# An attention and gated-convolution kernel on one core: loads held back by a second pass of its planner, memsets, weight conversion and small column copies put elsewhere

## The chip, the cores and the metric

The kernel runs on one core of a Trainium2 chip. The core has a matrix engine (PE, TensorE), three engines for elementwise work (DVE, the VectorE; ACT, the ScalarE; POOL, the GpSimd), and SP, the SyncE, whose queue issues nearly all of the DMAs here. Every engine works through its own instructions in order and waits at semaphores for the others. The metric is the device time of one execution in microseconds (us).

## The reference

Two stages, for a batch of 4 with 12800 rows of 128 numbers each, float32. An attention through 49 agents, and a gated convolution over its output:

```python
def sm(a, b):
    s = scale * (a @ b.transpose(0, 2, 1))
    s = s - s.max(-1, keepdims=True)
    e = np.exp(s)
    return e / (e.sum(-1, keepdims=True) + 1e-09)
agent_v = sm(agents, k) @ v          # 49 x 128 for each batch
x = sm(q, agents) @ agent_v          # 12800 x 128
# gated convolution, 5 taps that look back in the sequence
for t in range(5):
    gate_pre += conv_w[t][None, None, :] * xp[:, t:t + S, :]   # xp: 4 zero rows, then x
gate = 1.0 / (1.0 + np.exp(-gate_pre))
out = (gate * (x @ w_val)) @ w_out
```

The three weight arrays come in one array `moe`, whose numbers are float64; the kernel loads it as pairs of 32-bit words and makes float32 of it by integer operations.

## The kernel before

**Tiling.** A batch is cut into 10 units of 1280 rows (40 units in all), two units are a segment of 2560 columns, and the convolution runs over 100 chunks of 512 columns (the last is done in two halves). For a unit of keys, PE makes scores (`key_scores`, L401, matmuls L381), ACT copies them from PSUM to `ks` (L407), and DVE takes their maxima (`kmx`, L416). When all ten units of a batch are there, `key_max` makes one bias from the maxima, ACT takes exponentials (L476), DVE transposes them in blocks (`eT`, L391), and PE sums the values with them (`av`, L485). `fold_weights` then multiplies the agents' values into the weights of the convolution (`gw` L546, `wst`, `stat`), so that x itself is never formed: PE multiplies the attention weights with folded matrices.

**Queries.** For a unit of queries (`queries`), PE makes scores (L381), DVE transposes them (`sT`) and takes maxima (`qmx`), POOL subtracts (`qw` L755), ACT takes exponentials (L763), DVE sums and normalises (L768 to L777). The result goes to `pt` as float16 pieces: the high part (ACT L784), a repeated part (POOL L790) and the low part (POOL L798). `pt` is then transposed into a segment buffer `x1` (named x_0 to x_3 in traces) by a DMA transposition (L839; the first four units by PE, L853). The first four columns of a segment are the last four of the segment before; POOL copies them (`halo`, L823, or zeroes them at the start of a batch, L820).

**The fourth part, x2.** Nineteen of the 49 rows have a second low part for which `x1` has no room. Their five shifted copies are copied by two DMAs (`shifts`, L888) from rows of `x1` into `x2`, which has 128 partitions of 2560 columns with the 95 copied rows from partition 32 on; the partitions around them have to be zero, and POOL zeroes them once at the start (L275, L276).

**A chunk.** `gates`: five matmuls for the taps (L926) and one for x2 (L930), then a tanh on ACT (L939). `values`: two matmuls (L953, L957), then `h` on DVE (L966), its float16 part `hh` on ACT (L972) and the rest `hl` on POOL (L977). `project`: three matmuls (L996, L997 on `hh`, L998 on `hl`), a scaled copy on ACT (L1010), and for each pair of chunks a DMA to the output (L1025).

**What sets the order.** PE's order is a list written out by hand (`order`, L1092). Every other engine's order comes from `Plan`: each step is added with its engine, an estimated duration and the keys that it reads and writes; `Plan.order` (L96) replays the program once with these durations and, where several steps of an engine could run, takes the one with the longest tail of work behind it. DMAs are steps too; the ones on SP's queue stand there in the order of their planned starts. Loads go into a ring of eleven buffers (`load`, L359): a load may be planned as soon as the work on the load eleven places earlier is done. The weights (`weights`, L284) are one DMA and 13 operations on DVE; `urge=1e3` puts the DMA ahead of everything.

## Time and profile before

| | |
|---|---|
| time, three runs | 425.37, 426.81, 592.71 us; median 426.81 us |
| profiled execution: time, span | 425.08 us, 423.0 us |
| busy: PE, DVE, ACT, POOL | 400.9, 302.1, 301.5, 250.3 us |
| mean granted TensorE clock | 0.987 |
| moved by DMA | 127.63 MB, mean 302 GB/s |

The profile is one execution. Its span reaches from the first to the last instruction; the execution's own time is 2.08 us longer. A row of a timeline gives the start, the duration, the engine, the line, what is written from what, and in brackets how long the engine had been idle before and what ended that. A row of the waits gives the engine and line that waited, who released it, the sum in us, how often, and the longest. A row of the windows gives busy time and number of instructions for PE, its weight loads, DVE, ACT and POOL, then the granted PE clock, the DMA share and GB/s. SPq stands for SP's queue: the duration there is that of issuing the DMA, not of the transfer.

### The profile page before, as it was taken

Reading aid. Unit: us, or ns where it says so; the run is one execution under the profiler, and the core shown is the slowest. Engines: PE = TensorE matmul, PEld = TensorE weight load, DVE = VectorE, ACT = ScalarE, POOL = GpSimd, SP = SyncE. Lnnn points to the kernel's source line nnn. Section 1 sums busy time; section 2 is a strip of 40 time slices with the busy share of each in tenths; the row PEclk is TensorE's granted clock in tenths of the full one; section 3 lists DMA queues with packets and bytes.
Section 4 is the critical chain, followed back from the end, with each engine's and each line's share of the span. In section 5 each row is a group of like instructions: output and inputs, shape, how many; then the busy total and the mean of one; then the engine's idle time right before and its main releaser. Section 6 shows DMA issues by size and latency. Waiting matters only on the chain.

```text
span 423.0 us, 10093 instructions
## 1 busy us (share of the span) xinstructions
PE 400.9 (95%) x3907; PEld 194.3 (46%) x3907; DVE 302.1 (71%) x566; ACT 301.5 (71%) x521; POOL 250.3 (59%) x309
## 2 busy tenths in 40 slices
PE   4769999999999999999999999999999899999996
PEld 2239444336555443445555444344555444344443
DVE  6978899876885978676796775758766568676231
ACT  2446558779957677678886686779876467788776
POOL 9502558665677566555577564655476267887553
PEclk9969999999999999999999999999999989999999
DMA  8999999999999999999999999999999967655633
GB/s 319 417 418 413 352 381 363 293 323 311 414 317 288 376 350 340 377 284 307 362 350 316 319 229 364 309 310 254 318 415 315 235 177 168 192 164 176 198 128 124
DMA packets 75130, 127.63 MB, mean 302 GB/s; under 512 B 50466, under 2 KB 50850, under 8 KB 75084
## 3 DMA queue, kind: packets, MB, share of 16 engines
q1 hardware_dynamic: 74940, 126.87, 95.2%
q8 instruction: 30, 0.49, 0.6%
q10 hardware_dynamic: 144, 0.13, 0.2%
q14 instruction: 16, 0.13, 0.1%
HBM read 79.25 MB, written 26.21 MB: 249 GB/s over the span
## 4 chain that ended last, share of the span: by engine, by line
PE 81%; DVE 11%; DMA 3%; ACT 2%; POOL 2%; issue 1%; POOLq 0%; DVEq 0%
PE gate L926 24%; PE sc L381 18%; PE av L485 9%; PE val L953 5%; PE out L996 5%; PE gate L930 5%; PE val L957 5%; PE out L997 5%; PE out L998 5%; DVE ob L301 2%; DVE kmx L416 2%; DMA x<-pt 2%; DVE qw L777 1%; DVE h L966 1%; DMA ob<-moe 1%
## 5 line engine op out<-in xcount | busy, mean ns | idle before, releaser
L977 POOL TENSOR_TENSOR hl<-h,hh 128x512 f16<-128x512 f32 (+1 forms) x101 | 116.8, 1158 | 85.6 <-ACT hh L972 85.5
L926 PE MATMUL gate<-x,stat 128*128 128x512 f16 (+1 forms) x500 | 125.3, 381 | 0.4 <-ACT th L939 0.2
L966 DVE SCALAR_TENSOR_TENSOR h<-th,val 128x512 f32<-128x512 f32 x100 | 67.8, 678 | 62.9 <-PE out L997 27.0
L381 PE MATMUL sc<-ld,ag_sb 128*32 128x320 f32 x1280 | 102.0, 447 | 9.6 <-DMA ld<-kT 8.9
L939 ACT ACTIVATE th<-gate,unscale 128x512 f32<-128x512 f32 x100 | 68.5, 685 | 30.7 <-PE gate L930 29.4
L1010 ACT ACTIVATE ob<-out,oscale 128x512 f32<-128x512 f32 x98 | 67.4, 688 | 22.2 <-PE out L998 21.7
L926 PEld LDWEIGHTS <-stat 128*128 128x128 f16 x505 | 46.3, 98 | 63.7 <-issue 14.4
L972 ACT CAST hh<-h 128x512 f16<-128x512 f32 (+1 forms) x101 | 61.7, 611 | 15.9 <-DVE h L966 15.5
L381 PEld LDWEIGHTS sc<-ld,ag_sb 128*32 128x32 f32 x1280 | 36.5, 111 | 61.5 <-issue 25.2
L755 POOL TENSOR_TENSOR qw<-sT,qmx 128x490 f32<-128x490 f32 x40 | 41.4, 1035 | 34.8 <-DVE qmx L750 34.7
L485 PE MATMUL av<-ld,eT 128*32 128x129 f32 (+1 forms) x1400 | 48.0, 274 | 0.0
L485 PEld LDWEIGHTS av<-ld,eT 128*32 128x32 f32 (+1 forms) x1400 | 44.4, 113 | 6.9 <-issue 2.5
L798 POOL TENSOR_TENSOR pt<-qw,pt 128x490 f16<-128x490 f32 x40 | 44.8, 1120 | 1.0 <-ACT pt L784 0.8
L407 ACT COPY ks<-sc 128x640 f32<-128x640 f32 x40 | 27.6, 691 | 23.7 <-PE sc L381 18.4
L391 DVE STREAM_TRANSPOSE sT<-sc 128x640 f32<-128x640 f32 x40 | 33.5, 837 | 13.0 <-PE sc L381 12.3
L476 ACT ACTIVATE e<-ks,kbias 128x320 f32<-128x320 f32 x80 | 39.2, 555 | 3.0 <-DVE kbias L462 1.9
L998 PE MATMUL out<-hl,wo 128*128 128x512 f16 x98 | 37.1, 379 | 2.5 <-POOL hl L977 2.5
L790 POOL TENSOR_SCALAR pt<-qw 128x240 f16<-128x240 f32 x80 | 27.5, 365 | 20.0 <-DVE qw L777 20.0
L391 DVE STREAM_TRANSPOSE eT<-e 128x640 f32<-128x640 f32 x40 | 33.3, 839 | 7.5 <-ACT e L476 4.7
L953 PE MATMUL val<-x,stat 128*128 128x512 f16 x100 | 37.9, 379 | 0.2 <-DVE wo L733 0.2
L930 PE MATMUL gate<-x,stat 128*128 128x512 f16 x100 | 38.0, 380 | 0.0
L957 PE MATMUL val<-x,stat 128*128 128x512 f16 x100 | 37.8, 378 | 0.0
(132 smaller groups left out, 432.9 us busy)
## 6 DMA issues: line engine op xcount, KB each, us to landing
ld<-kT SPq DMA_DIRECT2D x40, 640.0 KB
ld<-qT SPq DMA_DIRECT2D x40, 640.0 KB
ld<-vP SPq DMA_DIRECT2D x39, 645.0 KB
outT<-ob SPq DMA_DIRECT2D x48, 512.0 KB
x<-x SPq DMA_DIRECT2D x18, 325.0 KB
x<-x SPq DMA_DIRECT2D x18, 150.0 KB
outT<-ob SPq DMA_DIRECT2D x3, 256.0 KB
x<-x SPq DMA_DIRECT2D x4, 162.5 KB
```

Of the source, the lines that this page charges most:

```text
L381: nc.tensor.matmul(out=out[g * BLK : (g + 1) * BLK, j, 0:GT], lhsT=ag_sb[:, b, j * BLK : (j + 1) * BLK], rhs=src[:, g * GT : (g + 1) * GT] ...
L391: nc.vector.transpose(out=out.rearrange("p n (j i) -> p j n i", j=2), in_=in_.rearrange("p j (n i) -> p j n i", i=BLK),)
L485: nc.tensor.matmul(out=av[o + j : o + j + cols, 0 : C + 1], lhsT=et[:, n, j : j + cols], rhs=vt[:, n, :], start=(u == 0 and n < 2), stop=( ...
L926: nc.tensor.matmul(out=pg, lhsT=stat[:, k, :], rhs=x1[:, c : c + w], start=(k == 0), stop=False,)
L930: nc.tensor.matmul(out=pg, lhsT=stat[:, TAPS + 1, :], rhs=x2[:, o2 : o2 + w], start=False, stop=True,)
L939: lambda: nc.scalar.activation(out=th, in_=pg, func=AF.Tanh, scale=unscale[:, 0:1]),
L953: nc.tensor.matmul(out=pv, lhsT=stat[:, TAPS, :], rhs=x1s[(b * NCH + n0 // CH) // 5 % NX][:, PAD + o2 : PAD + o2 + w], start=True, stop=False,
L957: nc.tensor.matmul(out=pv, lhsT=stat[:, TAPS + 2, :], rhs=x2[:, o2 : o2 + w], start=False, stop=True,)
L966: lambda: nc.vector.scalar_tensor_tensor(out=h, in0=th, scalar=1.0, in1=pv, op0=ALU.add, op1=ALU.mult),
L972: "act", 0.16 + 0.42 * scale, lambda: nc.scalar.copy(out=hh, in_=h),
L977: lambda: nc.gpsimd.tensor_tensor(out=hl, in0=h, in1=hh, op=ALU.subtract),
L1010: lambda: nc.scalar.activation(out=ob[:, o : o + w], in_=po, func=AF.Copy, scale=oscale),
```

## The change

Five edits, in the planner and in what is planned.

1. **Held loads.** `Plan.order` replays twice. From the first replay it takes, for each load, the earliest planned start of a step that uses it; in the second replay the load can't start earlier than `HOLD` = 13 planned us before that. PE's order stays as it was, row for row.
2. **Row copies of 12 and 7.** The nineteen rows of x2 are cut into 12 (first 2, every 4) and 7 (first 0, every 4) in place of 13 (first 0, every 4) and 6 (first 6, every 8); the two copies have 60 and 35 rows of five shifts in place of 65 and 30. The six further repeated rows of `pt` become 28, 32 to 48.
3. **Preceding columns later.** `halo` of a segment is added behind the POOL work on `pt` of that segment's second unit (it reads that key), no longer right behind the copies of the segment before.
4. **x2 zeroed elsewhere.** DVE zeroes the first 32 partitions as 32-bit words, ACT the last 32 by copying a zero column; both are planned steps. POOL's six memsets are gone.
5. **Weights behind values.** The DMA of `moe` loses its `urge`, and the 13 operations are planned with 0.43 us each.

**DVE, from the transpositions of the last exponentials to the fold of batch 0.** `eT` is the transposition whose result the value matmuls wait for, `ob` the buffers in which the weights are converted, `qsm`, `qr`, `qw` a unit of queries, `av2`, `den`, `avT` the fold. Before:

```order
L391 STREAM_TRANSPOSE eT1_83<-e1_81 128x2x10x32
L391 STREAM_TRANSPOSE eT2_84<-e0_80 128x2x10x32
L391 STREAM_TRANSPOSE eT0_82<-e1_81 128x2x10x32
L768 TENSOR_REDUCE qsm0_93<-qw0_89 128x10
L769 SCALAR_TENSOR_TENSOR qsm0_93<-qsm0_93,tiny_146 128x10
L772 RECIPROCAL qr0_95<-qsm0_93 128x10
L777 TENSOR_TENSOR qw0_89<-qw0_89,qr0_95 128x490
L524 COPY av2_169<-av_139 128x129
L539 TENSOR_SCALAR den_170<-out_138 128x49
L540 RECIPROCAL den_170<-den_170 128x49
L541 TENSOR_TENSOR avT_171<-out_138,den_170 128x49
```

Now:

```order
L412 STREAM_TRANSPOSE eT0_82<-e1_81 128x2x10x32
L322 TENSOR_SCALAR ob1_121<-ob0_120 128x261
L798 TENSOR_TENSOR qw0_89<-qw0_89,qr0_95 128x490
L337 CAST ob1_121<-ob1_121 128x261
L322 TENSOR_SCALAR ob1_121<-ob1_121 128x261
L339 SCALAR_TENSOR_TENSOR ob1_121<-ob1_121 128x261
L545 COPY av2_165<-av_139 128x129
L343 TENSOR_TENSOR ob1_121<-ob1_121 128x261
L322 TENSOR_SCALAR ob1_121<-ob0_120 128x261
L560 TENSOR_SCALAR den_166<-out_138 128x49
L561 RECIPROCAL den_166<-den_166 128x49
L562 TENSOR_TENSOR avT_167<-out_138,den_166 128x49
```

The conversion (rows on `ob`) stood ahead of and among the keys' maxima, at the start of DVE's program; now five of its 13 operations stand between the last `eT` rows just ahead of this piece, four ahead of `av2`, two between `av2` and `avT`, and the last two behind `avT`.

**POOL, around the second segment of batch 3.** `pt0` and `pt1` are the two units of a segment, `x1_0` its buffer, `x1_3` the segment before, `hl` what the chunks' last matmul waits for. Before:

```order
L790 TENSOR_SCALAR pt0_97<-qw0_89 128x10x24
L790 TENSOR_SCALAR pt0_97<-qw0_89 128x10x6
L798 TENSOR_TENSOR pt0_97<-qw0_89,pt0_97 128x10x49
L823 COPY x1_0_101<-x1_3_104 128x4
L977 TENSOR_TENSOR hl0_117<-h0_111,hh0_114 128x512
L977 TENSOR_TENSOR hl1_118<-h1_112,hh1_115 128x512
L546 TENSOR_TENSOR gw_173<-avT_171,moe_sb_167 128x245
L755 TENSOR_TENSOR qw1_90<-sT1_86,qmx1_88 128x490
L977 TENSOR_TENSOR hl2_119<-h2_113,hh2_116 128x512
```

Now:

```order
L819 TENSOR_TENSOR pt0_97<-qw0_89,pt0_97 128x10x49
L998 TENSOR_TENSOR hl1_118<-h1_112,hh1_115 128x512
L567 TENSOR_TENSOR gw_169<-avT_167,moe_sb_163 128x245
L776 TENSOR_TENSOR qw1_90<-sT1_86,qmx1_88 128x490
L998 TENSOR_TENSOR hl2_119<-h2_113,hh2_116 128x512
L710 TENSOR_SCALAR wo_172<-moe_sb_163,unscale1_131 128x128
L998 TENSOR_TENSOR hl0_117<-h0_111,hh0_114 128x512
L819 TENSOR_TENSOR pt1_98<-qw1_90,pt1_98 128x10x49
L811 TENSOR_SCALAR pt1_98<-qw1_90 128x10x24
L811 TENSOR_SCALAR pt1_98<-qw1_90 128x10x6
L846 COPY x1_0_101<-x1_3_104 128x4
```

The copy of the preceding columns has moved from ahead of two `hl` to behind the work on `pt1`, past four `hl`.

**SP's queue, at a transposition in batch 1.** `ld` are the ring's buffers, `x1_3<-pt2` is the transposition of the same unit in both. Before:

```order
L374 DMA ld0_61<-qT 128x1280
L1025 DMA outT<-ob2_122 128x1024
L888 DMA x20_105<-x1_2_103 65x1x2560
L888 DMA x20_105<-x1_2_103 30x1x2560
L374 DMA ld1_62<-kT 128x1280
L374 DMA ld2_63<-kT 128x1280
L374 DMA ld3_64<-qT 128x1280
L1025 DMA outT<-ob3_123 128x1024
L839 DMA_TRANSPOSE x1_3_104<-pt2_99 128x10x128
L374 DMA ld4_65<-vP 128x1290
```

Now:

```order
L909 DMA x20_105<-x1_2_103 60x1x2560
L909 DMA x20_105<-x1_2_103 35x1x2560
L395 DMA ld8_69<-kT 128x1280
L1046 DMA outT<-ob3_123 128x1024
L860 DMA_TRANSPOSE x1_3_104<-pt2_99 128x10x128
L395 DMA ld9_70<-kT 128x1280
L395 DMA ld10_71<-qT 128x1280
L1046 DMA outT<-ob0_120 128x512
L395 DMA ld0_61<-qT 128x1280
L860 DMA_TRANSPOSE x1_3_104<-pt3_100 128x10x128
```

Before, the loads up to buffer 3 stand ahead of this transposition and the next is that into buffer 4; now the next is that into buffer 9, which is six loads less ahead.

The diff:

```diff
--- before.py
+++ after.py
@@ -34,8 +34,8 @@
 NDUP = 30
 X2R = 19
 X2B = 32
-FOURS = 13
-X2CUTS = ((0, FOURS, 0, 4, 0.45), (FOURS, X2R, 6, 8, 0.25))
+FOURS = 12
+X2CUTS = ((0, FOURS, 2, 4, 0.45), (FOURS, X2R, 0, 4, 0.25))
 
 
 NLOAD = 11
@@ -61,6 +61,7 @@
 BACKLOG = 3.0
 LANES = 8
 LAND = 1.4
+HOLD = 13
 
 QS = 256.0
 WS = 64.0
@@ -76,11 +77,13 @@
 
 
     def __init__(self):
-        self.steps, self.urge = [], []
+        self.steps, self.urge, self.early = [], [], {}
         self.wrote, self.read = {}, {}
 
-    def add(self, engine, us, fn, reads=(), writes=(), moved=0.0, key=None, urge=0.0):
+    def add(self, engine, us, fn, reads=(), writes=(), moved=0.0, key=None, urge=0.0, early=None):
         i = len(self.steps)
+        if early is not None:
+            self.early[i] = early
         need = set()
         for x in reads:
             need |= self.wrote.get(x, set())
@@ -94,6 +97,15 @@
         self.urge.append(urge)
 
     def order(self):
+        self.replay({})
+        users = {i: [] for i in self.early}
+        for j, s in enumerate(self.steps):
+            for i in s[3]:
+                if i in users:
+                    users[i].append(self.start[j])
+        return self.replay({i: min(users[i]) - self.early[i] for i in users})
+
+    def replay(self, hold):
         n = len(self.steps)
         after = [[] for _ in range(n)]
         last = None
@@ -116,7 +128,7 @@
         wire = 0.0
         lanes = [0.0] * LANES
         left = [len(s[3]) for s in self.steps]
-        at = [0.0] * n
+        at = [hold.get(i, 0.0) for i in range(n)]
         queues = {e: [] for e in engines}
         pe = [i for i, s in enumerate(self.steps) if s[0] == "pe"]
         here = 0
@@ -261,6 +273,7 @@
     fold = const.tile([P, AP_], F32, name="fold")
     ag_sb = const.tile([P, B, AP_], F32, name="ag_sb")
     tiny = const.tile([P, NBLK], F32, name="tiny")
+    zero = const.tile([P, 1], F16, name="zero")
     nc.scalar.dma_start(out=ag_sb, in_=agT)
     make_identity(nc, ident)
     make_identity(nc, ident16)
@@ -271,9 +284,7 @@
     nc.vector.memset(x1s[0][:, 0:PAD], 0.0)
     for t in wst_sb:
         nc.gpsimd.memset(t[:, TAPS + 1 :, :], 0.0)
-    for t in x2s:
-        nc.gpsimd.memset(t[0:X2B], 0.0)
-        nc.gpsimd.memset(t[P - BLK :], 0.0)
+    nc.vector.memset(zero, 0.0)
 
     moe_sb = const.tile([P, NW], F32, name="moe_sb")
     wval_sb = moe_sb[:, 0:C]
@@ -284,8 +295,18 @@
     def weights():
 
 
+        for i, t in enumerate(x2s):
+            keys = [("x2", i, h, c[0]) for h in (0, UNIT) for c in X2CUTS]
+            add("dve", 1.4, lambda t=t: nc.vector.memset(t[0:X2B].bitcast(I32), 0), (), keys)
+            add(
+                "act", 2.0,
+                lambda t=t: nc.scalar.copy(
+                    out=t[P - BLK :], in_=zero[P - BLK :].to_broadcast([BLK, SEG])
+                ),
+                (), keys,
+            )
         if moe.dtype == F32:
-            add("dma", 0.4, lambda: nc.sync.dma_start(out=moe_sb, in_=moe), (), ["moe"], 0.4, urge=1e3)
+            add("dma", 0.4, lambda: nc.sync.dma_start(out=moe_sb, in_=moe), (), ["moe"], 0.4)
         else:
 
             i0, i1 = (t.bitcast(I32) for t in obs[0:2])
@@ -336,10 +357,10 @@
                 lambda: nc.sync.dma_start(
                     out=raw, in_=moe.bitcast(I32).rearrange("p (n two) -> p n two", two=2)
                 ),
-                (), ["raw"], 0.65, urge=1e3,
+                (), ["raw"], 0.65,
             )
             for fn in ops:
-                add("dve", 0.35, fn, ["raw"], ["bits"])
+                add("dve", 0.43, fn, ["raw"], ["bits"])
             add("dve", 0.43, whole, ["bits"], ["moe"] + [("ob", i, o) for i in range(2) for o in (0, CH)])
         add(
             "dve", 0.13,
@@ -372,7 +393,7 @@
         for d, f, keys in parts:
             add(
                 "dma", 0.4, lambda d=d, f=f: nc.sync.dma_start(out=d, in_=f), (), keys,
-                1.57 / len(parts),
+                1.57 / len(parts), early=HOLD,
             )
 
     def score_matmuls(b, src, out):
@@ -579,16 +600,16 @@
         ghi = wst[:, 0:TAPS, 0:A]
         vhi = wst[:, TAPS, 0:A]
 
-        def pick(x, first, every):
-            return x[:, first:A:every] if len(x.shape) == 2 else x[:, :, first:A:every]
+        def pick(x, first, every, n):
+            return (x[:, first:A:every] if len(x.shape) == 2 else x[:, :, first:A:every])[..., 0:n]
 
         def lows(low, full, hi, less):
 
 
             for out, first, every, n in (
-                (low[0], 1, 2, ODD), (low[1], 2, 8, NDUP - ODD), (low[2], 0, 4, FOURS), (low[3], 6, 8, X2R - FOURS),
+                (low[0], 1, 2, ODD), (low[1], 28, 4, NDUP - ODD), (low[2], 2, 4, FOURS), (low[3], 0, 4, X2R - FOURS),
             ):
-                less(out, pick(full, first, every), pick(hi, first, every))
+                less(out, pick(full, first, every, n), pick(hi, first, every, n))
 
         def rest(out, full, s, hi):
             dve.scalar_tensor_tensor(
@@ -786,9 +807,9 @@
         )
 
         def again():
-            for o, n, first, every in ((2 * A, ODD, 1, 2), (2 * A + ODD, NDUP - ODD, 2, 8)):
+            for o, n, first, every in ((2 * A, ODD, 1, 2), (2 * A + ODD, NDUP - ODD, 28, 4)):
                 nc.gpsimd.tensor_scalar(
-                    out=pt[:, :, o : o + n], in0=w[:, :, first : A - 1 : every],
+                    out=pt[:, :, o : o + n], in0=w[:, :, first : A : every][:, :, 0:n],
                     scalar1=1.0, scalar2=0.0, op0=ALU.mult, op1=ALU.add,
                 )
 
@@ -800,6 +821,9 @@
             ),
             [("qw", g % NPT), (*p_, 0)], [(*p_, 1)],
         )
+        if g % 2 and g > SINGLE + 1:
+            halo(g // 2, [(*p_, 1)])
+
     def on_pe(b, u):
         g = b * NU + u
         return g < PE_FIRST or (g < (B - 1) * NU and g % TURN in PE_TURNS)
@@ -814,19 +838,16 @@
         i = s % NX
         return [(x, i, h) for h in halves for x in ("x1", "x1b")] + [("x1h", i)] * (0 in halves)
 
-    def halo(s):
+    def halo(s, read=()):
         to = x1s[s % NX][:, PAD - HALO : PAD]
         if s * 2 % NU == 0:
             fn = lambda: nc.gpsimd.memset(to, 0.0)
-            read = []
         else:
             fn = lambda: nc.gpsimd.tensor_copy(
                 out=to, in_=x1s[(s - 1) % NX][:, PAD + SEG - HALO : PAD + SEG]
             )
-            read = [(x, (s - 1) % NX, 1) for x in ("x1", "x1b")]
-
-        read.append(("x2", (s - 1) % 3, UNIT, 0))
-        add("pool", 0.1, fn, read, [("x1h", s % NX)])
+        keys = [(x, (s - 1) % NX, 1) for x in ("x1", "x1b")]
+        add("pool", 0.19, fn, list(read) + keys, [("x1h", s % NX)])
 
     def transposes(b, u):
         g = b * NU + u
@@ -891,8 +912,8 @@
                 ),
                 src, [("x2", s % 3, o + i * UNIT, r0) for i in range(n)], us * n,
             )
-        if g % 2 and (g + 1) // 2 < B * NU // 2:
-            halo((g + 1) // 2)
+        if g % 2 and g < SINGLE:
+            halo(g // 2 + 1)
 
 
     chunks = [(t // NCH, t % NCH * CH, CH) for t in range(NT - 1)]
```

## The prediction

> **What bounds the kernel now.** The page's busy line and the chain of work that ended last say PE:
>
> ```profile
> PE 400.9 (95%) x3907; PEld 194.3 (46%) x3907; DVE 302.1 (71%) x566; ACT 301.5 (71%) x521; POOL 250.3 (59%) x309
> PE 81%; DVE 11%; DMA 3%; ACT 2%; POOL 2%; issue 1%; POOLq 0%; DVEq 0%
> ```
>
> PE's order is the same row for row after the change, so its work is the same, and only its idle time and its clock can move. The table of windows shows where it idles (first number behind the length: PE's busy time):
>
> ```profile
> 0.00:30.00 30.00, 17.46 (x186) 7.17 (x188) 23.48 (x34) 10.88 (x17) 15.20 (x16) 0.89 0.96 383
> 30.00:40.00 10.00, 10.00 (x186) 10.00 (x184) 9.21 (x15) 7.59 (x16) 1.02 (x1) 1.00 1.02 414
> 40.00:60.00 20.00, 17.83 (x207) 8.35 (x203) 16.64 (x45) 10.48 (x18) 11.57 (x20) 1.00 1.00 366
> 60.00:330.00 270.00, 269.52 (x2863) 130.78 (x2861) 202.19 (x375) 204.99 (x357) 165.48 (x207) 1.00 1.08 329
> 330.00:340.00 10.00, 7.51 (x56) 3.54 (x57) 4.47 (x11) 4.32 (x8) 2.67 (x5) 1.00 1.05 212
> 340.00:344.00 4.00, 4.00 (x20) 1.30 (x13) 3.23 (x15) 2.12 (x6) 3.05 (x5) 0.57 1.01 218
> ```
>
> Idle are 12.5 us of the first 30, 2.2 us between 40 and 60, 0.5 us in the 270 us that follow, and 2.5 us before 340; then PE is busy at a clock of 0.57. So there are two places to gain at, the start and 330 to 344, and 270 us in which there is only something to lose.
>
> **The preceding columns: 4.0 us.** The chain at 330 us, rows of PE, and the sum of the copy's waits on POOL:
>
> ```profile
> 330.31 7.25 DMA x<-pt
> 337.62 0.19 POOL x L823
> 338.97 0.38 PE L998 MATMUL out<-hl,wo 128*128 128x512 f16 x1 [2.49 <-POOL hl L977]
> 340.76 2.31 PE L926 MATMUL gate<-x,stat 128*128 128x512 f16 x5
> 322.86 1.24 PE L926 MATMUL gate<-x,stat 128*128 128x512 f16 x5
> POOL x L823 <- DMA x<-pt: 19.5, 5, 7.3
> ```
>
> The 4-column copy waited 7.3 us for a transposition, two `hl` were queued behind it on POOL, and PE stood 2.49 us for the first of them. Behind the stop PE ran at half clock: 0.57 granted over 4.0 us is 1.7 us of work lost; PE's own rows bear that out, 2.31 us in place of 1.24 for five matmuls, with slower ones behind. I take 1.5, since the window is cut generously. The change puts this copy behind POOL's work on the segment's second unit, four `hl` later. By then the transposition that it waits for is a unit old, and the copy itself costs the same 0.19 us. What waits for it next are the row copies, which need the transposition of that second unit anyway, and this starts only after the same POOL work. So 2.5 + 1.5 = 4.0 us go. The other four of the five waits (12.2 us) reached PE nowhere that the windows show, and bring nothing. What is late next is `gw` (L546) on POOL, which comes 7 us earlier as well.
>
> The page "TensorE: Matmul & The Clock Gate" of the Trainium skill, section "What's actually happening", states that the clock halves after an idle window of about 3.4 us. By it a stop of 2.5 us need not cost clock, the term would be 2.5 and the sum below 1.5 us higher; here the clock did halve, and the trace decides.
>
> **The start: +0.5 us.** Rows of the timeline of the first 43 us:
>
> ```profile
> 0.74 0.40 SPq L336 DMA_DIRECT2D ob<-moe  x1
> 4.28 2.68 DVE L301 TENSOR_SCALAR ob<-ob 128x261 int32<-128x261 int32 x2 [2.68 <-DMA ob<-moe]
> 8.39 0.69 ACT L407 COPY ks<-sc 128x640 f32<-128x640 f32 x1 [5.96 <-PE sc L381]
> 9.16 2.29 POOL L276 MEMSET x<- 32x2560 f16 x1
> 9.31 0.43 DVE L307 TENSOR_TENSOR ob<-ob 128x261 int32<-128x261 int32 x1
> 18.41 0.29 DVE L301 TENSOR_SCALAR ob<-ob 128x261 int32<-128x261 int32 x1
> 21.48 6.60 SPq L374 DMA_DIRECT2D ld<-vP  x5
> 21.55 1.28 PE L381 MATMUL sc<-ld,ag_sb 128*32 128x320 f32 x16 [1.78 <-DMA ld<-kT]
> 24.62 0.82 DVE L416 TENSOR_REDUCE kmx<-sc 128x2 f32<-128x640 f32 x1
> 25.47 0.69 ACT L407 COPY ks<-sc 128x640 f32<-128x640 f32 x1 [4.95 <-DVE kmx L416]
> 27.34 2.95 ACT L476 ACTIVATE e<-ks,kbias 128x320 f32<-128x320 f32 x6 [1.17 <-DVE kbias L462]
> 29.39 0.33 SPq L374 DMA_DIRECT2D ld<-qT  x1
> 37.26 0.33 SPq L374 DMA_DIRECT2D ld<-qT  x1
> 38.29 2.50 PE L485 MATMUL av<-ld,eT 128*64 128x129 f32 x42
> 40.82 0.29 DVE L524 COPY av<-av 128x129 f32<-128x129 f32 x1 [0.61 <-PE av L485]
> 42.90 0.60 POOL L546 TENSOR_TENSOR gw<-avT,moe_sb 128x245 f32<-128x245 f32 x1 [0.87 <-DVE avT L541]
> ```
>
> What comes earlier: keys and values. 0.64 us is what the 267 KB of `moe` (128 rows of 261 words of 8 bytes) take at the 414 GB/s of the window 30 to 40; the keys no longer stand behind them. The last `kmx` begins at 24.62 because DVE, late from the conversion, has a row of them to catch up (3.71 us for five without a pause), though the last scores began at 21.55 and took 1.28: straight behind them it could begin at 22.83, 1.8 us earlier. Together the exponentials can begin 2.4 us earlier, about 24.9.
>
> What holds it back. The loads: SP issues one when the eighth before it has landed, as the row at 21.48 shows: the last keys were eight places ahead of that load, and their scores began at 21.55. From 29.39 to 37.26 there are five loads, 1.57 us each. Eight places ahead of the one at 37.26 was the last but one load of values, so the last lands near 38.8. `moe` is still loaded ahead of that, so this doesn't move. Behind it PE has some ten matmuls at 60 ns (42 in 2.50 us), so the copy of `av`, 40.82 now, can begin at 39.4 at the earliest: at most 1.4 are to be had of the 2.4. And DVE: it is busy 9.21 of the 10 us from 30 to 40, and gets eleven operations of the conversion into that stage and two behind `avT`. Undisturbed one costs 0.29 (18.41) to 0.43 us (9.31), so all 13 cost 3.8 to 5.6 us, and I take 4.5, of which 3.8 for the eleven. Against that stand the 2.4 us by which the stage begins earlier and some 0.8 of idle time in it: +0.6. The last two operations cost 0.3 to 0.4 each, and `gw` waits for them too, +0.7; but PE has the next units' scores to do there, which hide most of that. I take +0.5 in all, between −1.4 (the loads' bound, conversion hidden) and +2.4 (5.6 for all 13 at the upper price, less 2.4 and 0.8).
>
> The zeroing of `x2` is hidden: ACT stands idle 5.96 us ahead of its first copy of keys and 4.95 ahead of the last, and a copy of 2560 columns costs at most four times the 0.69 of one with 640, 2.8 us, two at the first place and one at the second. DVE's three memsets, each 1280 words where POOL's took 2.29 for 2560 halves, stand ahead of the first `kmx`, which waits for ACT's copy at 8.39. If this cover were gone, 1 us of keys would be late, and 24.9 would become 25.9. With POOL's memsets gone, nothing stretches the conversion there any more (2.68 for two, against 0.29 for one).
>
> **Held loads: +0.5 us.** Rows of a load of keys in batch 1 and its use, of a transposition between them, and the waits on SP's queue:
>
> ```profile
> 147.96 0.38 SPq L374 DMA_DIRECT2D ld<-kT  x1
> 160.04 5.79 SPq L839 DMA_TRANSPOSE x<-pt  x1
> 172.75 2.36 PE L381 MATMUL sc<-ld,ag_sb 128*32 128x320 f32 x32
> SPq L1025 <- ACT ob L1010: 40.3, 19, 5.6
> SPq L839 <- POOL qw L755: 22.1, 5, 6.5
> ```
>
> `moe` was issued at 0.74 and its first reader began at 4.28: 3.5 us for a transfer with the queues empty. A load at the pace of 1.57 us then needs about 3.5 − 0.64 + 1.57, some 4.5 us (estimate). This load was issued 24.8 us ahead of its use; now it stands behind the transposition of 160.04, whose issue holds SP until 165.8, which leaves 6.9 us, and 2.4 beyond the 4.5. A hold of 13 planned us is thus enough where one transposition stands ahead, and not where SP waits at the same place for up to 5.6 (an output's result) or 6.5 us (POOL) as well. Behind a late load in SP's queue stand the next output and the next transposition; PE waits for the load at once, POOL's row copies for the transposition. The window 60 to 330 has 0.5 us of idle time, so every late load counts in full. What a hold can give, ring buffers that are filled less early, is worth nothing on PE there. I take +0.5, one load late by that; the bounds are 0 and +10.6 (first rival).
>
> **Nothing.** The row copies move 95 rows either way, in two DMAs, with 5 rows from one to the other: 0, and ±0.1 for SP's issue. The repeated rows of `pt` are as many as before. The tail's instructions stay.
>
> **Sum.** 425.08 − 4.0 + 0.5 + 0.5 = 422.1, on the scale of the profiled execution (span 423.0 and 2.08 around it). The two runs that agree were 425.37 and 426.81, so the median lies 1.7 above this execution and the faster run 0.3; I forecast 422.0.
>
> **The rivals.**
>
> *Late loads, slower.* If a held load stands behind a transposition of 5.8 us and a wait of 6.5, 13 − 12.3 = 0.7 us are left for 4.5: PE stands 3.8 us, and 1.5 of half clock behind it, as at 340: 5.3. One such place gives 427, two 432, three 438. It decides from where more than 13 − 4.5 = 8.5 us stand ahead of a load. For it: 24 waits of these two kinds, 119 loads. Against: the second plan knows of transpositions and of results, so that most waits fall behind the held load as well, and the largest waits of these rows may be ones that cost nothing now. 0.13, of which half for over 433.6.
>
> *DVE is blocked by POOL, no gain.* Two rows of one operation, and what stood beside the slow one:
>
> ```profile
> 318.05 0.66 DVE L777 TENSOR_TENSOR qw<-qw,qr 128x490 f32<-128x490 f32 x1
> 326.95 1.51 DVE L777 TENSOR_TENSOR qw<-qw,qr 128x490 f32<-128x490 f32 x1
> 326.77 1.16 POOL L977 TENSOR_TENSOR hl<-h,hh 128x512 f16<-128x512 f32 x1 [1.28 <-ACT hh L972]
> 35.97 1.02 POOL L755 TENSOR_TENSOR qw<-sT,qmx 128x490 f32<-128x490 f32 x1 [19.89 <-DVE qmx L750]
> 40.93 1.09 POOL L798 TENSOR_TENSOR pt<-qw,pt 128x490 f16<-128x490 f32 x1
> ```
>
> With POOL at work, DVE's operation took 0.85 longer: it stood until POOL's was done. In the new place the conversion meets POOL's 1.02 on `qw`, two on `pt` and 1.09 behind them, 2.8 us in all. If these block it in full, the start is 0.5 + 2.8 = 3.3 us later, and 425 comes out. Against: POOL is busy only 1.02 of the 10 us from 30 to 40, and the conversion's merges with two inputs took 0.43 under a memset (9.31). The page "SBUF — State Buffer" of the Trainium skill, section "SBUF: two separate sides", states that the port pair DVE and GpSimd share is locked for a whole instruction, and that DVE operations with two SBUF inputs meet it only against GpSimd operations that read SBUF; by it the merges too would be blocked in the new place, where POOL reads, and the row at 9.31, which ran under a memset, does not speak against it. 0.15.
>
> *The start gains in full.* The conversion fits into idle time of DVE: −1.4, and nearly all of the 2.2 us of PE's gaps between 40 and 60 go with it, 2.1, since `gw` and what follows come before PE has run out of scores. With the 4.0 that gives 425.08 − 4.0 − 1.4 − 2.1 = 417.6. For it: keys earlier by 2.4. Against: 9.21 of 10. 0.15, of which a third below 416.6.
>
> *The stop at 339 stays.* If the copy in its new place waits too, or the row copies behind it come late to x2's matmul, the 4.0 don't come: 426. It would need another transposition of over 7 us there. 0.05.
>
> **How the numbers follow.** My sum has 0.52. The range reaches from the third rival, 417, over the second and fourth to one late place of the first with a median 1.5 higher, 428.5; left out are the rest of the first rival and what lies below the third. 2%, 8.5 us, is what can be told from no change here: below 416.6 lies a third of the third rival, 0.05; above 433.6 half of the first, 0.06; 0.89 between.
>
> **What would show it.** POOL's wait at the copy of preceding columns gone, PE's last matmul of a chunk without its 2.49 us near 339, and a granted clock of 1.00 in 340 to 344. Exponentials from about 24.9, the copy of `av` at about 41, `gw` at 43 to 44; DVE's conversion in operations of 0.29 to 0.43 (longer ones are the second rival). PE idle at most 1 us in 60 to 330, with waits for `ld` no longer than 0.5; waits of 2 us and more there are the first rival, and would make the prediction wrong most.

## The result

The changed kernel took 429.1 us in the median of 7 runs (427.5 to 432.75); the kernel before, run beside it, 423.49 us (420.95 to 426.81 but for one). The ratio is 1.0132, with a 95% interval from 1.0091 to 1.0172: slower, by less than 2%. The forecast was 422.0, the range 417 to 428.5. The profiled execution has a span of 428.1 us, 5.1 more than before.

The page of the changed kernel, busy line and chain:

```profile
PE 400.7 (94%) x3907; PEld 194.1 (45%) x3907; DVE 296.7 (69%) x570; ACT 307.3 (72%) x524; POOL 236.9 (55%) x303
PE 72%; DMA 19%; DVE 4%; issue 1%; ACT 1%; SPq 0%; POOL 0%; POOLq 0%; DVEq 0%
```

PE's work is the same (400.7 for 400.9), and DMA's share of the chain went from 3% to 19%. The windows (length; busy time of PE, its weight loads, DVE, ACT, POOL; granted clock, DMA share, GB/s) say where PE stands:

```profile
0.00:30.00 30.00, 21.20 (x248) 10.95 (x250) 17.39 (x27) 21.39 (x27) 1.64 (x10) 0.94 0.95 382
30.00:40.00 10.00, 8.16 (x135) 7.22 (x131) 9.12 (x22) 4.61 (x10) 2.62 (x4) 1.00 1.03 412
40.00:60.00 20.00, 15.65 (x189) 7.22 (x189) 16.54 (x47) 9.25 (x17) 8.40 (x16) 1.00 0.92 332
60.00:330.00 270.00, 262.89 (x2765) 126.37 (x2758) 199.18 (x368) 199.41 (x349) 160.23 (x199) 1.00 1.05 314
330.00:340.00 10.00, 10.00 (x119) 5.37 (x121) 4.98 (x10) 6.51 (x12) 5.57 (x8) 1.00 1.08 276
340.00:344.00 4.00, 4.00 (x32) 1.93 (x25) 2.56 (x7) 2.30 (x5) 2.80 (x5) 1.00 0.84 108
```

Two things happened as the change meant them. From 330 to 344 PE no longer stops, and the clock stays at 1.00. In the first 30 us PE does 3.7 us more. And one thing was paid: between 60 and 330 PE is idle 7.1 us, where it was 0.5. The timeline of PE has the places; the last brackets name what PE waited for:

```profile
42.45 0.42 PE L590 MATMUL val<-avT,moe_sb 128*128 128x49 f32 x2 [1.29 <-DVE moe_sb L353]
52.23 0.38 PE L951 MATMUL gate<-x,stat 128*128 128x512 f16 x1 [2.23 <-DMA x<-x]
57.98 2.36 PE L402 MATMUL sc<-ld,ag_sb 128*32 128x320 f32 x32 [0.67 <-DVE sT L412]
167.36 1.28 PE L402 MATMUL sc<-ld,ag_sb 128*32 128x320 f32 x16 [1.71 <-DMA ld<-kT]
273.10 1.28 PE L402 MATMUL sc<-ld,ag_sb 128*32 128x320 f32 x16 [1.33 <-DMA ld<-kT]
276.19 1.28 PE L402 MATMUL sc<-ld,ag_sb 128*32 128x320 f32 x16 [1.05 <-DMA ld<-qT]
308.44 1.31 PE L506 MATMUL av<-ld,eT 128*32 128x129 f32 x40 [1.89 <-DMA ld<-vP]
395.06 1.24 PE L947 MATMUL gate<-x,stat 128*128 128x512 f16 x5 [0.18 <-ACT th L960]
```

With four smaller waits (0.16, 0.35, 0.30, 0.38) the loads cost 7.2 us behind 60. The row at 57.98 answers to the one at 57.14 before, so the start costs 0.8. The row at 395.06 answers to one at 390.50, 4.6 later. What is left over for the stop at 339, its half clock and a wait of 0.29 at 286 that is gone too is 0.8 + 7.2 + 0.3 (a small wait for ACT at 95) − 4.6 = 3.7. The last 0.5 of the 5.1 lie behind it, at the very end: the last output took 2.1 us from issue to landing, not 1.7, which is most of it.

How a late load looks in the chain of waits (start, length, engine; the length at a DMA runs from its issue to its landing):

```profile
157.07 10.15 DMA ld<-kT
...
258.76 8.67 DMA ld<-kT
269.65 8.03 DMA ld<-kT
...
296.67 11.62 DMA ld<-vP
```

These loads were not only issued late; they took 8 to 12 us each. The prediction had counted 4.5.

### The profile page after: what moved, and what is told of

It is laid out like the page before. It is cut to its first block, busy times and chain, and to the rows that moved or that the text cites. A ratio compares the mean times of both kernels' runs of the same rounds, so it can differ in the third digit from the quotient of the medians.

```text
span 428.1 us, 10102 instructions
## 1 busy us (share of the span) xinstructions
PE 400.7 (94%) x3907; PEld 194.1 (45%) x3907; DVE 296.7 (69%) x570; ACT 307.3 (72%) x524; POOL 236.9 (55%) x303
## 4 chain that ended last, share of the span: by engine, by line
PE 72%; DMA 19%; DVE 4%; issue 1%; ACT 1%; SPq 0%; POOL 0%; POOLq 0%; DVEq 0%
PE gate L947 22%; PE sc L402 16%; DMA ld<-kT 11%; PE av L506 8%; DMA ld<-vP 5%; PE val L974 5%; PE out L1017 4%; PE val L978 4%; PE gate L951 4%; PE out L1018 4%; PE out L1019 4%; DMA x<-x 2%; DMA ld<-qT 1%; DVE h L987 1%; PE sc L874 0%
## 5 line engine op out<-in xcount | busy, mean ns | idle before, releaser
L402 PE MATMUL sc<-ld,ag_sb 128*32 128x320 f32 x1280 | 102.2, 448 | 12.5 <-DMA ld<-kT 10.4
L506 PE MATMUL av<-ld,eT 128*32 128x129 f32 (+1 forms) x1400 | 49.3, 275 | 3.7 <-DMA ld<-vP 3.4
L437 DVE TENSOR_REDUCE kmx<-ks 128x2 f32<-128x640 f32 x39 | 31.6, 814 | 11.7 <-ACT ks L428 11.5
```

The lines of the kernel that those rows point to most:

```text
L402: nc.tensor.matmul(out=out[g * BLK : (g + 1) * BLK, j, 0:GT], lhsT=ag_sb[:, b, j * BLK : (j + 1) * BLK], rhs=src[:, g * GT : (g + 1) * GT] ...
L506: nc.tensor.matmul(out=av[o + j : o + j + cols, 0 : C + 1], lhsT=et[:, n, j : j + cols], rhs=vt[:, n, :], start=(u == 0 and n < 2), stop=( ...
```

## The experiments

The table is worked out from the profiles and times of all kernels that ran. *PE idle* is 320 us less PE's busy time in the window 60 to 380, *loads* the part of it that PE waited for `ld`, *start* the time at which the 61st gate matmul begins, with the start of the program and the first fold behind it. *Ratio* is to the kernel before, run on the same chip.

| kernel | edits | ratio (95%) | PE idle | loads | start |
|---|---|---|---|---|---|
| before | – | 1 | 3.0 | 0 | 93.6 |
| changed | all five, hold 13 | 1.0132 (1.0091–1.0172) | 7.5 | 7.2 | 94.9 |
| no hold | all but 1 | 0.9958 (0.9923–0.9993) | 0.2 | 0 | 95.5 |
| hold 26 | all five | 0.9937 (0.9909–0.9964) | 0.2 | 0 | 96.4 |
| hold 17 | all five | 1.0057 (1.0018–1.0096) | 2.2 | 1.0 | 97.7 |
| hold alone | 1 | 0.9950 (0.9913–0.9987) | 0.9 | 0.7 | 93.8 |
| preceding columns alone | 3 | 0.9926 (0.9895–0.9957) | 1.0 | 0 | 94.6 |
| hold, columns | 1, 3 | 0.9968 (0.9925–1.0011) | 0.2 | 0 | 93.8 |
| hold, zeroing, weights | 1, 4, 5 | 1.0099 (1.0062–1.0135) | 5.3 | 4.9 | 94.4 |
| columns, zeroing | 3, 4 | 0.9936 (0.9898–0.9975) | 3.0 | 0 | 93.0 |
| one place of SP's queue | all five | 1.0115 (1.0059–1.0171) | 5.1 | 4.8 | 94.7 |
| twelve rows of SP's queue | all five | 1.0045 (1.0009–1.0080) | 3.8 | 3.5 | 94.3 |
| transposition planned with 3.3 us | all five | 0.9951 (0.9912–0.9991) | 1.1 | 0.2 | 94.2 |
| columns, zeroing, hold 13 | 1, 3, 4 | 0.9941 (0.9905–0.9977) | 5.0 | 4.7 | 92.7 |
| columns, zeroing, hold 20 | 1, 3, 4 | 0.9894 (0.9843–0.9946) | 0.2 | 0 | 92.3 |
| columns, zeroing, hold 26 | 1, 3, 4 | **0.9860 (0.9818–0.9903)** | 0.2 | 0 | 92.6 |

PE idle and loads are of one profiled execution each, the ratio of 6 to 12 timed runs. In the row of columns, zeroing and a hold of 13 the profiled execution (427.36 us) was the longest of its kernel, whose median is 423.46; its waits are an upper end.

**Is it the hold?** Four kernels. The hold taken out of the changed kernel:

```diff
-        return self.replay({i: min(users[i]) - self.early[i] for i in users})
+        return self.replay({})
```

> The changed kernel with the hold taken out (the second plan is made without it); the other four edits stay. Theory H (held loads land too late): the waits of PE for loads after 60 us, 7.2 us in the changed kernel, all but vanish (under 0.5 us), and what is left is 0.8 us lost at the start and 3.7 gained at the preceding columns: about 421 us of span, a ratio to before of 0.990 to 0.996. Rival S (the four other edits shift the work so that loads come late anyway, by new orders on SP): waits for loads of 3 us and more stay, ratio 1.00 to 1.01.

The hold twice as long in it:

```diff
-HOLD = 13
+HOLD = 26
```

> The changed kernel with a hold of 26 planned us in place of 13. A load took 8 us from issue to landing in the median (up to 13) in both traces, and 4 to 6.5 us of a transposition can stand ahead: 26 covers both. Theory H: no wait of PE for loads after 60 us over 0.3 us, time as without the hold within 1 us, ratio 0.990 to 0.996. Rival (any hold spoils the order on SP, whatever its length, since loads then stand among transpositions and outputs): half of the 7.2 us stays, ratio about 1.00 to 1.01.

The kernel before with edit 1 alone:

```diff
     def order(self):
+        self.replay({})
...
+        return self.replay({i: min(users[i]) - self.early[i] for i in users})
...
-                1.57 / len(parts),
+                1.57 / len(parts), early=HOLD,
```

> The kernel before with the hold of 13 alone. Theory H: waits of PE for loads of 5 to 9 us in all after 60 us, the stop of 2.5 us for the preceding columns stays: ratio 1.012 to 1.022. Rival S (the hold hurts only beside the other edits): waits under 2 us, ratio 0.998 to 1.005.

And the kernel before with edit 3 alone:

```diff
-        if g % 2 and (g + 1) // 2 < B * NU // 2:
-            halo((g + 1) // 2)
+        if g % 2 and g < SINGLE:
+            halo(g // 2 + 1)
...
+        if g % 2 and g > SINGLE + 1:
+            halo(g // 2, [(*p_, 1)])
```

> The kernel before with the later copy of the preceding columns alone. My step of the prediction: the stop of 2.49 us at 339 and the half clock behind it go, 3.5 to 4 us less, ratio 0.990 to 0.993; POOL's waits at that copy (19.5 us) go to under 3 us. Rival: the copy or what follows waits elsewhere, and PE stops for it at another place: ratio 0.996 to 1.002.

Without the hold the waits for loads were gone and the ratio was 0.9958; with a hold of 26 they were gone as well, 0.9937, some 8 us below the same kernel with 13. So the hold's length makes the changed kernel slow, and holding as such does not. Theory H held in both. With the hold of 13 *alone* both theory H's 1.012 and the waits of 5 us failed to come: the window 60 to 380 of that kernel has 0.85 us of idle time, and the ratio was 0.995. Its row of the windows, and the one wait for a load in PE's timeline:

```profile
60.00:380.00 320.00, 319.15 (x3174) 152.66 (x3172) 241.09 (x456) 242.49 (x422) 202.69 (x253) 1.00 1.04 310
```

```profile
165.24 1.28 PE L393 MATMUL sc<-ld,ag_sb 128*32 128x320 f32 x16 [0.68 <-DMA ld<-kT]
```

Its stop at 339 was gone too, though the copy of the preceding columns stood where it did: the transposition that it waits for landed at 329.6 us, not 337.6, with three loads issued between 305 us and it, not seven. Rival S had the waits right, though not the ratio, for which it had said 0.998 at least. The hold hurts only beside other edits. The later copy by itself gave 0.9926, 3.1 us of 424, close to the 3.5 to 4 expected; POOL's waits at it went from 19.5 to 0.3 us, with a new wait of PE of 0.84 us for a row copy at 332 as a part of the difference.

**What do loads need?** The semaphore events of the traces give each load's issue and landing; I set them against the first matmul that uses the load (us; lead is the time between landing and use; loads used after 60):

```
kernel              issue to landing     lead
                    median   longest     least   median   under 1 us
before               7.9      12.5        4.9     18.6        0
changed              8.0      13.1        0.0      2.8       19
hold alone           7.9      12.3        0.1      4.1        6
hold, columns        7.7      13.2        0.5      4.3        1
all, no hold         8.4      13.5        5.7     21.0        0
all, hold 26         7.9      12.4        5.8     12.1        0
```

Holding hardly changes how long a load takes: with the hold as without, some four other transfers of SP's queue are under way beside it (4.1 to 4.4 on average in four of these traces). What it takes away is the lead. A hold of 13 leaves a median of some 4 us at best. The hold alone works with 0.1 us at its tightest load, so a few us of delay on SP's queue can decide.

**Which delay?** First the edits beside the hold, in the kernel before: hold, zeroing and weights (edits 1, 4, 5); hold and columns (1, 3); and columns and zeroing without a hold (3, 4).

```diff
 # edit 4
-    for t in x2s:
-        nc.gpsimd.memset(t[0:X2B], 0.0)
...
+            add("dve", 1.4, lambda t=t: nc.vector.memset(t[0:X2B].bitcast(I32), 0), (), keys)
...
 # edit 5
-                (), ["raw"], 0.65, urge=1e3,
+                (), ["raw"], 0.65,
```

> The kernel before with the hold, x2 zeroed elsewhere and the weights behind the values; SP's queue has the two transpositions side by side as in the changed kernel. Theory O: PE waits 5 us and more for loads between 160 and 310, ratio 1.005 to 1.018, the stop for the preceding columns may stay. Rival (the halo edit, by POOL's order, makes the transpositions late): waits under 1.5 us, ratio 0.995 to 1.002.

> The kernel before with the hold and the later copy of the preceding columns; SP's queue keeps the two transpositions apart. Theory O: waits for loads under 1.5 us, ratio 0.990 to 0.997. Rival (the halo edit makes the transpositions late): 4 us and more of waits for loads, ratio 1.005 to 1.015.

> The kernel before with the later copy of the preceding columns and x2 zeroed by DVE and ACT, with the weights still loaded first and no hold: the parts of the change that should gain without those that cost. Theory: the conversion runs early in DVE's idle time and undisturbed, exponentials begin at about 24, gw has no wait for the weights (1.3 us in the changed kernel), and the stop at 339 is gone: ratio 0.986 to 0.992. Rival (the last values land near 38.7 in any case, and the row copies behind them): the start gains nothing, ratio as with the later copy alone, 0.990 to 0.996.

Hold, zeroing and weights reproduce the loss (1.0099, 4.9 us of waits for loads); hold and columns don't (0.9968, none). So the loss needs neither the later copy of the preceding columns nor the new cut of the row copies, which the slow kernel of the two didn't have. Zeroing and weights were not run with the hold one at a time. Columns and zeroing came to 0.9936, in the rival's interval and not in the theory's: it starts the second stage at 93.0, only 0.6 us earlier than the kernel before, and waits 1.66, 0.65 and 0.41 us for row copies. With a longer hold (the last two kernels below) these three waits are gone, which points to loads ahead of the copies.

Where the two queues differ: the hold alone first, then the changed kernel, SP's own timeline (the second number is how long SP was held by the issue):

```profile
221.77 4.85 SPq L851 DMA_TRANSPOSE x<-pt  x1
226.67 0.90 SPq L386 DMA_DIRECT2D ld<-qT  x1
227.66 0.37 SPq L386 DMA_DIRECT2D ld<-kT  x1
228.14 2.96 SPq L851 DMA_TRANSPOSE x<-pt  x1
231.20 1.05 SPq L1037 DMA_DIRECT2D outT<-ob  x2
232.34 0.40 SPq L386 DMA_DIRECT2D ld<-kT  x1
```

```profile
224.58 8.09 SPq L860 DMA_TRANSPOSE x<-pt  x2
232.77 0.54 SPq L395 DMA_DIRECT2D ld<-qT  x1
233.40 0.37 SPq L395 DMA_DIRECT2D ld<-kT  x1
233.87 0.38 SPq L1046 DMA_DIRECT2D outT<-ob  x1
```

In the changed kernel two transpositions stand side by side and hold SP for 8.1 us, and the two loads go out some 4 us later against their use (8.5 us ahead of it, not 12.5). I moved the second transposition behind these two loads, and in another kernel I gave twelve rows from there the order of the hold alone; the edit of the first:

```diff
+    turn = plan.order()
+    turns = [i for i in turn if plan.steps[i][0] == "dma" and plan.steps[i][4] == 2.4]
+    late = turns[17]
+    k = turn.index(late)
+    stop = [j for j in range(k, len(turn)) if turn[j] in plan.early][1]
+    turn.remove(late)
+    turn.insert(stop, late)
-    for i in plan.order():
+    for i in turn:
```

> The changed kernel, all five edits and the hold of 13 as they are, with one transposition (the eighteenth, issued behind another one at 224.6 us, the two holding SP for 8.1 us) moved two places back on SP's queue, behind the two loads that stood behind it; that is where it stands when the hold is made alone. Theory O (the hold leaves a slack of 1 to 4 us, and this one place on SP's queue uses it up: SP is some 4 us late from there on): the waits of PE for loads at 267 to 278 and 305 to 308, 5.1 us in all, go to under 1.5 us, ratio to before 0.996 to 1.004. Rival H (13 is too short whatever the order): the waits between 260 and 310 stay at 4 us and more, ratio 1.010 or more.

> The changed kernel with twelve rows of SP's queue, from the eighteenth transposition on, in the order that the hold alone gives them: the second of the two transpositions behind two loads, and a load and an output ahead of the two row copies, behind which the load came 2.2 us late at 249 us when the transposition alone was moved. Theory O (the order at this place uses up the small slack): PE waits under 2 us for loads in all after 60 us (those at 166 and 353 may stay), ratio to before 0.997 to 1.005. Rival (the slack is used up at many places, and a wait that is taken away at one comes at the next): 4 us and more in all, ratio 1.008 or more.

One place moved: the waits at 267 to 278 and 305 to 308 went from 5.1 to 0.8 us, as theory O said, but a wait of 2.24 us came at 249, for a load that stands behind two row copies, which now went out at 239.7 and not at 235.4, and the clock halved behind it. The time stayed (1.0115, in rival H's interval; theory O had said 1.004 at most). Twelve rows: no wait between 168 and 300 any more, 1.0045, inside its expectation, though 3.5 us of waits stayed at 167, 303 and 350, not under 2. The order at this place is about half of the loss; the other half comes from other places with as little lead. The rival (used up at many places) is right for that half.

**How much longer must the hold be?**

```diff
-HOLD = 13
+HOLD = 17
```

> The changed kernel with a hold of 17 planned us in place of 13. The loads land 0 to 6 us ahead of their use in the changed kernel; 4 us more should lift the smallest leads to 3 or 4 us. Theory H (13 is just below the point from which a hold costs): no wait of PE for a load over 0.5 us after 60 us, ratio 0.990 to 0.998, as with 26. Rival (the leads don't follow the hold, since SP stands behind transpositions): 2 to 5 us of waits stay, ratio 1.000 to 1.010.

4 us more took the waits for loads from 7.2 to 1.0 (one of 0.82 us, where theory H allowed none over 0.5), but the ratio was 1.0057, not under 0.998. The tightest loads still landed only 0.04 us ahead of their use, and 11 of them less than 1 us, with a median lead of 5.3: the lead doesn't follow the hold load by load, as the rival said. The rest of the time is at the start, which is 2.8 us later than with 13 in the profiled execution, and there most of it is the clock: 0.50 granted from 43.3 to 46.7 us and from 53.5 to 56.9, where the changed kernel had 1.00. The same 32 matmuls, with a hold of 17 and then with 13:

```profile
42.80 4.05 PE L402 MATMUL sc<-ld,ag_sb 128*32 128x320 f32 x32
```

```profile
42.80 2.36 PE L402 MATMUL sc<-ld,ag_sb 128*32 128x320 f32 x32
```

Whether the other executions with a hold of 17 had these slow stretches isn't known.

**Why is 13 too short?** The planner counts 1.4 us of SP's time for a transposition. The view of that line says otherwise (ns: shortest, median, longest), in the changed kernel:

```profile
L860 SPq DMA_TRANSPOSE x<-pt x36: 1336/3330/6574, 74.5 to 399.1; - x36
```

So 13 planned us are fewer where transpositions stand ahead. In one kernel the planner counts 3.3, with everything else as in the changed kernel; another has the hold of 13 without the move of the weights:

```diff
 # the price of a transposition
-                "dma", 1.4,
+                "dma", 3.3,
                 lambda: nc.sync.dma_start_transpose(
 # the kernel before with edits 1, 3 and 4
+HOLD = 13
```

> The changed kernel with all five edits and the hold of 13; the planner counts 3.3 us of SP's time for a transposition in place of 1.4 (a median issue held SP for 3.3 us, the longest 6.6). Theory P (the hold is a planned time, and the plan is too fast where transpositions stand ahead): loads are planned ahead of transpositions that they stood behind, PE waits under 2 us for loads after 60 us in place of 7.2, ratio 0.992 to 1.003. Rival (the price of the issue isn't it; transfers of 8 us and more are): 4 us and more of waits stay, ratio 1.007 or more.

> The kernel before with the later copy of the preceding columns, x2 zeroed by DVE and ACT, the weights first as before, and the hold of 13. Theory W (moving the weights behind the values shifts the planned times, and with them SP's order, so that a hold of 13 gets too short): PE waits under 1.5 us for loads after 60 us, ratio 0.982 to 0.992. Rival Z (the zeroing or the halo copy does it, or the hold of 13 is too short whenever the start is earlier): 4 us and more of waits for loads, ratio 0.995 or more.

With 3.3 us planned, the hold of 13 works with all five edits: 0.2 us of waits for loads and a ratio of 0.9951, against 1.0132. Theory P held, and this is the clearest of the runs: nothing that is computed, no buffer and no hold was changed, only the price of one step in the plan. The plan then puts loads ahead of transpositions that they had stood behind: on SP's queue 38 of the 120 loads have one or two transpositions fewer ahead of them, and none has more. The lead is not longer for it (3.1 us in the median, 2.8 in the changed kernel), but 6 loads land less than 1 us ahead of their use, not 19. Leaving the weights first gave 0.9941, just outside theory W's interval and under rival Z's; its profiled execution, the longest of the twelve, has waits of 4.7 us for loads, rival Z's mark. A hold of 13 can thus be too short there as well, with the weights first; how much the other executions waited isn't known.

**The start, and a kernel that beats both.** The wait of 2.23 us at 52.23 is for the first row copies. Set beside the loads that SP had issued ahead of them (from 37.5 on), and their landing by the trace's events:

```
kernel               loads ahead     row copies issued   landed    PE waited
before                    0            44.1, 45.2         49.9       0
columns, zeroing, 26      0            42.8, 43.9         50.1       1.07
changed                   1            43.8, 44.8         52.2       2.23
all, hold 26              2            43.9, 44.9         53.8       2.47
```

PE's row for the first of these matmuls, with all edits and a hold of 26, and then with columns, zeroing and 26:

```profile
53.88 0.39 PE L951 MATMUL gate<-x,stat 128*128 128x512 f16 x1 [2.47 <-DMA x<-x]
```

```profile
50.14 0.39 PE L951 MATMUL gate<-x,stat 128*128 128x512 f16 x1 [1.07 <-DMA x<-x]
```

With the weights behind the values SP's order has one or two loads ahead of these row copies; they go out at 38, and the copies land 2 to 4 us later behind them. All sixteen traces agree: the later of the two copies landed between 49.1 and 50.3 us with no load ahead, between 51.3 and 52.2 with one, between 53.0 and 53.8 with two. The start of the exponentials does not tell these kernels apart (23.3 us with all edits and a hold of 26, 23.6 in the changed kernel, 24.0 with columns, zeroing and 26). The earlier start went into the late copies and some 0.8 us for the weights (PE waits 1.29 us for them at the row of 42.45, and 0.49 at the same matmul where they are loaded first). With all edits and a hold of 26 the clock was 0.50 from 43.0 to 46.4 us besides. So I kept the weights first and the row copies as they were, and took the later copy, the zeroing and a longer hold:

```diff
 # the kernel before with edits 1, 3 and 4, and
+HOLD = 26
 # or
+HOLD = 20
```

> The kernel before with the later copy of the preceding columns, x2 zeroed by DVE and ACT, the weights first as before, and a hold of 26. Theory: as with these two edits alone the second stage starts some 2 us earlier than in before, and the waits for row copies that this had without a hold (0.65, 1.66 and 0.41 us) go, since loads no longer stand ahead of them: some 418 us of span, ratio 0.982 to 0.990. Rival (the waits for row copies come from the transpositions, not from loads ahead of them): 2 to 3 us of them stay, ratio 0.991 to 0.996.

> The same with a hold of 20. Theory: leads of 3 us and more for all loads, row copies not behind loads: as with 26 within 0.3 %, or a little better at the row copies. Rival: PE waits 1 to 3 us for loads again, ratio 0.5 % above that of 26.

With 26 the ratio is 0.9860 (0.9818 to 0.9903), as expected, the best of all that ran: median 419.32 us beside 424.46 for the kernel before. No load or row copy is waited for after 60:

```profile
60.00:380.00 320.00, 319.83 (x3176) 152.73 (x3174) 239.47 (x456) 243.09 (x424) 203.22 (x251) 1.00 1.05 307
```

With 20 it is 0.9894, not told apart from 26.

## Why the prediction was wrong

**Held loads: wrong, by its size.** The term was +0.5 and measured 7.2. The step that failed is the 4.5 us for a load from issue to landing, worked out from the very first transfer of the program, with empty queues. A load among the others takes 8 us in the median, and did so in the trace of before (7.9). At its start it took still longer, and the rows quoted in the prediction show it: SP issued the load at 37.26 only when one issued at 24.6 had landed, 12.6 us later. With 8, the first rival's point of decision is 13 − 8 = 5 us ahead of a load, not 8.5, and the transposition of 5.79 us quoted there is enough by itself. The rival had the mechanism: late loads behind transpositions, ending slower. It had a chance of 0.13, and its price was of another form: not one or two stops of 5.3 us with half clock, but eight of 0.2 to 1.9 us, none with half clock. The bound of 10.6 held the 7.2; the range stopped at one such stop, 428.5, 0.6 short.

That the plan's us aren't the chip's was the second part: the term took 13 planned us for 13, and SP is held 3.3 us by a transposition that is planned with 1.4. The third was to price the edit by itself. For the hold alone +0.5 was about right (0.7 us of waits), though with loads of 8 us that was luck; beside the zeroing and the weights it was 4.9, beside all the others 7.2. What these edits change on SP's queue at one place accounts for about half of that. Which of the two does it, and how the other half comes about, stays open.

**The preceding columns: right.** −4.0 forecast, −3.7 from the two timelines, and 0.9926, some 3.1 us, by itself. POOL has no wait at that copy, the clock is 1.00 in 340 to 344. That the same stop goes with the hold alone, without this edit, was not foreseen: either of the two edits removes it when it is made by itself.

**The start: right in sum, wrong in its parts.** +0.5 forecast, +0.8 measured; that they agree is luck. The exponentials start at 23.6, 3.7 us earlier, not 2.4: the last scores began at 19.64 and not at 21.55, 1.9 us earlier where the prediction had 0.64, since the last keys landed at 19.5 and not at 21.4. The maxima, straight behind the scores, gave 1.7 of the 1.8 us that it had for them. The bound by the last values held: the copy of `av` is at 39.60, for 39.4 at the earliest. The two operations behind `avT` cost some 0.8 us of the 1.29 that PE waits there, since PE's next work, ahead of the scores that I had let cover them, multiplies these very weights (L590). The 2.23 us for row copies were not foreseen: a load that goes out earlier is in the way of them.

**DVE blocked by POOL: mostly not.** In the new place of the conversion:

```profile
38.55 0.42 DVE L322 TENSOR_SCALAR ob<-ob 128x261 int32<-128x261 int32 x1
39.00 0.43 DVE L339 SCALAR_TENSOR_TENSOR ob<-ob 128x261 f32<-128x261 f32 x1
39.09 1.29 POOL L819 TENSOR_TENSOR pt<-qw,pt 128x490 f16<-128x490 f32 x1
39.81 0.85 DVE L343 TENSOR_TENSOR ob<-ob 128x261 f32<-128x261 f32 x1
```

One operation with two inputs took 0.85 us, 0.42 more than the 0.43 of before, while POOL's ran; the others took 0.25 to 0.51. That is 0.5 us, not 2.8. The page "SBUF — State Buffer" of the Trainium skill, section "SBUF: two separate sides", lets a two-input operation of DVE wait for a GpSimd operation that reads SBUF; the row at 39.81 agrees.

**Zeroing and row cuts: right.** ACT's copies took up to 2.32 us in time that was free, and the slow pair of edits needs no row cuts.

## What to carry to other kernels

Price a transfer by what it takes among its neighbours, in the stage where it will run: here the price from the first transfer of the program, with empty queues, was 4.5 us against 8 measured. A lead far larger than the loads needed cost nothing at the loads themselves, and it covers a planner's wrong prices; shorten it only after comparing the plan's price of each step on that queue with the trace. And an edit that lets a transfer go out earlier puts it ahead of others: look at what then stands behind it in the same queue.

## What the runs showed of the hardware

Issuing a DMA transposition of the same shape held SP for 1.3 to 6.6 us in the changed kernel, 3.3 in the median (2.4 to 3.5 in the other traces), where the issue of an ordinary load took 0.4 us in the median.

A stop of PE didn't have one length from which the clock halved. The granted clock (third from the end of a row of the windows) in the 3.4 us behind three stops. Behind 1.88 us, in the kernel with hold, zeroing and weights:

```profile
307.40:310.80 3.40, 3.40 (x12) 1.18 (x10) 1.78 (x4) 0.69 (x1) 0.00 (x0) 0.51 1.08 239
```

Behind 2.24 us, in the one with one place moved:

```profile
249.60:253.00 3.40, 3.40 (x18) 1.02 (x11) 0.69 (x1) 1.20 (x2) 0.00 (x0) 0.50 1.01 380
```

Behind 2.34 us, in the one with twelve rows moved:

```profile
167.40:170.80 3.40, 3.40 (x27) 1.43 (x27) 1.47 (x3) 2.08 (x4) 0.12 (x1) 1.00 1.12 278
```

The first two halved it, the longest didn't; in the changed kernel 1.89 us at 308 didn't either. The traces' records of the granted clock show why. In each execution the clock changes only on a grid of steps of 3.413 us, whose place differs from one execution to the next (in the changed kernel it changes at 9.75, 23.41 and 26.82 us). What tells the cases apart is how long PE was idle within one step; the clock that follows is that of the next step:

```
kernel                     stop    idle in the step that has most of it    clock in the next
changed, at 308            1.89               1.72                            1.00
twelve rows, at 167        2.34               1.86                            1.00
hold, zeroing, weights     1.88               1.88                            0.50
before, at 339             2.49               1.91                            0.50
one place, at 249          2.24               2.24                            0.50
```

From 45 us to 12 us before the end, this holds in all sixteen traces: each of the four steps with 1.88 us or more idle was followed by one at half clock, and no step with 1.86 or less was (three had 1.86). Between 39 and 44 us, where PE has many short matmuls, 1.38 to 1.67 us idle in a step were followed by half clock in four traces, so idle time alone doesn't decide there. The page "TensorE: Matmul & The Clock Gate" of the Trainium skill, section "What's actually happening", speaks of a window of about 3.4 us that runs freely, and of half clock after an idle window. The grid of 3.413 us agrees with it; a window that is idle throughout was not needed, since 1.88 us of it were enough.
